# Moving a gain vector's load and transpose, one addition and one norm step in a fused attention and feed-forward kernel

## The chip, the cores and the metric

The kernel runs on one core of a Trainium2 chip. The metric is the device time of one execution in microseconds (us); a change of this kernel's time by less than 0.3% can't be told from none. The core has five instruction streams that run beside each other, each in its own order: the tensor engine (PE, with its weight loads listed apart as PEld), the vector engine (DVE), the scalar engine (ACT), GpSimd (POOL) and the sync engine (SP), which here only issues transfers; SPq is SP's queue of such issues. Semaphores order the streams among each other.

## The reference

Attention with normalised queries and keys is followed by a feed-forward block. Shapes: batch 8, 12 heads, sequence 448, head width 64; 3584 tokens, model width 768, inner width 1024.

```python
q_n, k_n = (rmsnorm(q, g_q), rmsnorm(k, g_k))      # x / sqrt(mean(x*x) + 1e-6) * g
scores = q_n @ k_n.T / sqrt(64)
attn = softmax(scores)
x = (attn @ v)                                     # (B,H,S,D) -> (B*S, H*D)
h = x @ w_in                                       # 768 x 1024
solu = h * softmax(h)
ln = (solu - mean) / sqrt(var + 1e-6) * g_ln
out = ln @ w_out                                   # 1024 x 768
```

The gain `g_ln` is 1024 numbers. The kernel multiplies it into `w_out` when it prepares that matrix, which is long after the attention stage has begun.

## The kernel before, in words

The work has three stages: attention, the product with `w_in` (L982), and the product with `w_out` (L1177). All that the change touches lies in the attention stage and, of that, in its first 75 us.

**Pairs and quads.** Two heads of one batch entry are a pair; there are 48 pairs, numbered from 0, and pairs 2m and 2m+1 (a and b in the code) make quad m. Each pair passes through these steps:

- `load(n)` (L634) fetches the pair's queries and keys by eight transfers on SP's queue; `load_v(m)` (L647, L651) fetches the values of a quad by three. Five buffers hold queries and keys.
- `squares(n)` (L656, ACT), `row_sums(n)` (L664, DVE), `fold_sums(m)` (L674, L675, POOL; for a whole quad) or `fold_one(n)` (L684, L685, DVE; for the early pairs), `rsqrt_seed` (L694, L695, ACT), `rsqrt_step` (L701 to L704, DVE), `normalise(n)` (L713, POOL), `qk_transpose(n)` (L723, DVE) and `gain(n)` (L727, ACT) turn them into the transposed, normalised operand qkT. This row of steps is called the chain of norms below. It goes from engine to engine, and it belongs to the quad after the one that the tensor engine is working on.
- `scores(n, kc)` (L812, PE) makes one block of scores for both heads, and `exponentials` (L802, ACT) takes its exponentials. A quad has seven such units: three of pair a, here called s0, s1 and s2; one for the last 64 keys of both pairs (`scores_last`, L825), here called last; and three of pair b, here called b0, b1 and b2.
- `add(n)` (L839, DVE) adds two of a pair's blocks of exponentials, so that the sums of rows cost fewer matmuls.
- `values_last` and `values` (L854, L865, PE) multiply with the values, `sums(m)` (L884, PE) adds up the exponentials, `inverse(m)` (L895, L896 on DVE, L903 on POOL) takes the reciprocals, and `divide(m)` (L910, L911, DVE) scales the result into `xo`, which `store_x` (L916) sends to memory.

**What sets the order.** The order is written by hand: the code runs under `manual_schedule`, and every engine executes its instructions in the order in which they are recorded. `unit(f)` records f and then whatever `later(...)` has made due. Three banks of the tensor engine's result memory (tag "t") are handed out in turn to the score units, to the sums sm and to the transpose pg below, so each of these must wait until the third one before it has been read.

**The gain vector.** `load_norm_gain()` issues two transfers on SP's queue (L469, 2 KB each) into `grow`. `norm_gain()` transposes `grow` on the tensor engine (L476, one matmul into a bank pg of tag "t") and copies the result to `gcol` on ACT (L477). Before the change the transfers are the last thing that quad 0 records, behind `load(6)`, `load(7)` and two transfers of `w_in` (L510); `norm_gain()` stands in quad 1 behind s1 and ahead of s2.

Of the kernel before, what the change touches and what calls it, by code (L numbers as in the profile page):

```python
# [366 lines left out]
def fast_path(  # L367
# [99 lines left out]
    def load_norm_gain():  # L467
        for i in range(2):
            nc.sync.dma_start(  # L469
                grow[i * HF : (i + 1) * HF].rearrange("c (g j) -> c g j", g=4),  # L470
                moe_g_ln.rearrange("(h g c j) -> h c g j", h=2, g=4, j=32)[i],
            )

    def norm_gain():
        pg = ps_t.tile([P, KF], FP32, tag="t", name="pg")
        nc.tensor.transpose(pg, grow, ident[0:KF, 0:KF])  # L476
        nc.scalar.copy(gcol[:, 0:KF], pg)  # L477
# [149 lines left out]
    def load(n):  # L627
        b, hp = divmod(n, NP)
        h0 = 2 * hp
        d = st[n] = {}  # L630
        d["qk"] = loads.tile([P, 2, NB, 32], FP32, tag="qk", name="qk", bufs=5)
        for s, src in enumerate((q, k)):
            for g in range(4):
                nc.sync.dma_start(  # L634
                    d["qk"][g * 32 : g * 32 + 32, s],
                    src[b, h0 + g // 2].rearrange("(b t) (x d) -> x t b d", t=32, x=2)[g % 2],
                )
# [15 lines left out]
    def squares(n):  # L653
        d = st[n]
        d["sq"] = work.tile([P, 2 * NB, 32], FP32, tag="sq", name="sq", bufs=2)
        nc.scalar.activation(d["sq"], d["qk"].rearrange("p s b d -> p (s b) d"), AF.Square)  # L656
# [3 lines left out]
    def row_sums(n):  # L660
        m, i = divmod(n, 2)
        if i == 0:
            norms[m] = {"part": small.tile([P, 2, 2 * NB], FP32, tag="part", name="part", bufs=2)}
        nc.vector.tensor_reduce(norms[m]["part"][:, i], st[n]["sq"], AX, OP.add)  # L664
# [139 lines left out]
    def scores(n, kc):  # L804
        d = st[n]
        s = ps_t.tile([P, 2, 512], FP32, tag="t", name="s")

        for c in range(0, P, D):
            for h in range(2):
                hh = slice(h * D, (h + 1) * D)  # L810
                keys = slice(NJ * c + kc, NJ * (c + D - 1) + kc + 1, NJ)
                nc.tensor.matmul(  # L812
                    s[c : c + D, h, 0:S], d["qkT"][hh, 1, keys], d["qkT"][hh, 0, :],
                    start=True, stop=True,
                )
        exponentials(d, kc, s)
# [19 lines left out]
    def add(n):  # L836
        d = st[n]
        d["es"] = work.tile([P, 2, S], FP32, tag="es", name="es")
        nc.vector.tensor_tensor(d["es"], d["E", 0], d["E", 1], OP.add)  # L839
# [433 lines left out]
    def unit(f, steps=4):  # L1273
        nonlocal now
        f()
        now += steps
        due = [x for x in todo if x[0] <= now]
        todo[:] = [x for x in todo if x[0] > now]
        for _, g in sorted(due, key=lambda x: x[0]):
            g()  # L1280
# [35 lines left out]
    load(3)  # L1316
    load_v(0)
    load(4)
    load(5)
    with tc.manual_schedule():  # L1320
        warm_up()
# [18 lines left out]
        for m in range(NQ):  # L1340
            a, b = 2 * m, 2 * m + 1

            def outputs():
                values_last(m)
                values(a)


            next1 = m + 1 < NQ
            next2 = m + 2 < NQ
            next3 = m + 3 < NQ  # L1350
            if m == 0:
                unit(lambda: scores(a, 0))
                normalise_rows(1, 0)
                normalise_rows(1, 1)
                unit(lambda: scores(a, 1))
                unit(lambda: scores(a, 2))
                for s in range(2):
                    transpose_rows(1, s)
                    take_rows(1, s)
                squares(2)  # L1360
                row_sums(2)
                fold_one(2)
                unit(lambda: scores_last(m))
                rsqrt_seed(norms["one", 2])
                rsqrt_step(norms["one", 2])
                normalise(2)
                add(a)
                unit(lambda: scores(b, 0))
                unit(lambda: scores(b, 1))
                unit(lambda: scores(b, 2))  # L1370
                squares(3)
                row_sums(3)
                qk_transpose(2)
                fold_one(3)
                gain(2)
                rsqrt_seed(norms["one", 3])
                add(b)
                rsqrt_step(norms["one", 3])
                normalise(3)
                load_v(1)  # L1380
                load(6)
                load(7)
                for _ in range(2):
                    load_next()
                unit(outputs)
                squares(4)
                row_sums(4)
                qk_transpose(3)
                gain(3)
                unit(lambda: values(b))  # L1390
                unit(lambda: sums(m))
                inverse(m)
                load_norm_gain()
                later(1, lambda m=m: divide(m))
                continue
            early = 2 < m and next1
            if early:
                rsqrt_seed(norms[m + 1])
                rsqrt_step(norms[m + 1])
                normalise(a + 2)  # L1400
                normalise(b + 2)
            for x in joins_at.get(m, ()):
                combine_in(x)
            if next1:
                load_v(m + 1)
            unit(lambda: scores(a, 0))
            store_x(m - 1)
            if early:
                qk_transpose(a + 2)
                if next3:  # L1410
                    load(a + 6)
            unit(lambda: scores(a, 1))
            if m == 1:
                squares(5)
                row_sums(5)
                fold_sums(2)
                norm_gain()
            if m == 2:
                rsqrt_seed(norms[m + 1])
                rsqrt_step(norms[m + 1])  # L1420
                normalise(a + 2)
                normalise(b + 2)
            unit(lambda: scores(a, 2))
            unit(lambda: scores_last(m))
            if m < 2:
                add(a)
            unit(lambda: scores(b, 0))
            if m == 1:
                rsqrt_seed(norms[m + 1])
                rsqrt_step(norms[m + 1])  # L1430
                normalise(a + 2)
                normalise(b + 2)
                load(a + 6)
                load(b + 6)
            if m == 2:
                qk_transpose(a + 2)
                load(a + 6)
            unit(lambda: scores(b, 1))
            if early or m == 2:
                qk_transpose(b + 2)  # L1440
                if next3:
                    load(b + 6)
            if m > 1:
                add(a)
            unit(lambda: scores(b, 2))
            if m == 1:
                qk_transpose(a + 2)
            scarce = m < 5
            if next2:
                squares(a + 4)  # L1450
                if not scarce:
                    squares(b + 4)
                row_sums(a + 4)
            if next1:
                gain(a + 2)
            if m == 1:
                add(b)
                qk_transpose(b + 2)
            if next1:
                gain(b + 2)  # L1460
            if scarce:
                squares(b + 4)
                if m > 1:
                    add(b)
            if next2 and m > 1:
                row_sums(b + 4)
                fold_sums(m + 2)
            if not scarce:
                add(b)
            add_more(a)  # L1470
            add_more(b)
            unit(outputs)
            step(m - 2)
            begin(m)
            step(m - 1)
            if m - 1 in sets:
                load_next()
            unit(lambda: values(b))
            if m == NQ - 1:
                block_sums(0, 0)  # L1480
                block_sums(0, 1)
                load_x(1)
            unit(lambda: sums(m))
            inverse(m)
            if m == 1:
                row_sums(b + 4)
                fold_sums(m + 2)
            if next1:
                later(1, lambda m=m: divide(m))
            if m == NQ - 2:  # L1490
                load_x(0)
                sizes(0)
# [191 lines left out]
```

## Time and profile before

| quantity | value |
|---|---|
| median of 3 runs | 831.3 us (830.87 to 833.21) |
| profiled execution, time | 830.15 us |
| profiled execution, span from first to last instruction | 827.9 us |
| mean granted clock of the tensor engine | 0.988 |
| PE busy | 800.3 us (97% of the span) |
| DVE, ACT, POOL busy | 671.0, 460.8, 463.8 us |
| quad 0's scores begin | 10.54 us |
| quads 1, 2, 3, 4: the first score unit begins | 26.18, 53.37, 67.52, 81.32 us |
| quads 1, 2, 3: L865 begins | 46.68, 60.83, 74.63 us |

The span is a little shorter than the profiled execution's own time; the 2.25 us between them lie before the first instruction and after the last. The last two rows of the table are starts of instructions in the timeline. From quad 4 on one quad takes 12.9 us. A timeline's row gives the start and the length in us, the engine, the line and operation, the tile written and read, the number of instructions merged into it, and in brackets how long the engine was idle before it and what ended that.

### The profile page before, as it was taken

What the parts mean: (1) busy time and instruction counts of PE and PEld (TensorE: products, weight loads), DVE (VectorE), ACT (ScalarE), POOL (GpSimd) and SP (SyncE); (2) the same over time, 40 slices, a digit from 0 to 9 for tenths busy, and PEclk for the clock granted to TensorE, in tenths of its full rate; (3) what the DMA queues carried; (4) which work ended last, traced back from release to release, by engine and by line L of the source; (5) the groups of instructions that cost most, each with busy time, mean ns of one, the idle gap of its engine ahead of it and who ended that gap; (6) DMA issues with size and microseconds to landing.
All of it is one profiled execution on the core that took longest, in us unless ns stands there. A gap on an engine that the chain in (4) does not pass through costs nothing.

```text
span 827.9 us, 14945 instructions
## 1 busy us (share of the span) xinstructions
PE 800.3 (97%) x5030; PEld 471.0 (57%) x5030; DVE 671.0 (81%) x1203; ACT 460.8 (56%) x757; POOL 463.8 (56%) x635
## 2 busy tenths in 40 slices
PE   8399999999999999999999999999899999999996
PEld 4133444444444444444444444444589999999996
DVE  5558988888788788579999999998996866966945
ACT  6377877778777786355656534443324464464420
POOL 1243465555555556523254358777477777877761
PEclk9799999999999999999999999999999999999999
DMA  7755878778777762434555444452457466375312
GB/s 136 179 105 117 200 157 193 150 164 182 150 182 157 155 140 84 127 90 127 151 138 169 127 121 115 119 151 74 133 172 239 139 225 222 126 248 192 133 58 82
DMA packets 271938, 122.74 MB, mean 148 GB/s; under 512 B 190444, under 2 KB 257004, under 8 KB 271852
## 3 DMA queue, kind: packets, MB, share of 16 engines
q1 hardware_dynamic: 256668, 111.79, 51.4%
q10 hardware_dynamic: 15184, 9.90, 4.2%
q8 instruction: 42, 0.69, 0.4%
q14 instruction: 44, 0.36, 0.1%
HBM read 84.94 MB, written 36.70 MB: 147 GB/s over the span
## 4 chain that ended last, share of the span: by engine, by line
PE 88%; DVE 4%; SPq 2%; POOL 2%; DMA 2%; issue 1%; ACT 0%; DVEq 0%; POOLq 0%
PE b L982 31%; PE A L1177 14%; PE o L865 12%; PE s L812 12%; PE B L1177 7%; PE sm L884 5%; PE C L1177 3%; PE s L825 2%; PE o L854 2%; SPq L634 2%; DMA grow<-in_moe_g_ln_dram 1%; DVE part L664 0%; POOL sums L1156 0%; DMA x<-in_k_dram 0%; POOL qkn L713 0%
## 5 line engine op out<-in xcount | busy, mean ns | idle before, releaser
L982 PE MATMUL b<-w_in,xg 128*128 128x512 f32 x336 | 151.2, 592 | 0.0
L802 ACT ACTIVATE E<-s 128x896 f32<-128x896 f32 x168 | 139.2, 935 | 17.6 <-PE s L812 16.6
L812 PE MATMUL s<-qkT 64*64 64x448 f32 x1152 | 121.6, 549 | 1.6 <-ACT E L802 0.9
L982 PE MATMUL b<-w_in,xsum 128*128 128x512 f32 x252 | 115.0, 592 | 0.0
L865 PE MATMUL o<-E,v 128*64 128x448 f32 x576 | 113.5, 543 | 0.0
L982 PEld LDWEIGHTS b<-w_in,xg 128*128 128x128 f32 x336 | 63.8, 190 | 80.2 <-issue 76.9
L713 POOL TENSOR_TENSOR qkn<-qk,ny 128x896 f32<-128x896 f32 x46 | 78.0, 1715 | 31.2 <-DVE ny L704 12.0
L674 POOL COPY ss<-part 32x56 f32<-32x56 f32 x88 | 42.6, 484 | 90.6 <-DVE part L664 87.7
L1177 PE MATMUL A<-w_out,sums 128*128 128x192 f32 x392 | 81.1, 330 | 4.0 <-ACT u L1189 2.6
L812 PEld LDWEIGHTS s<-qkT 64*64 64x64 f32 x1152 | 48.5, 163 | 60.1 <-ACT E L802 29.1
L982 PEld LDWEIGHTS b<-w_in,xsum 128*128 128x128 f32 x252 | 47.9, 190 | 60.3 <-issue 57.4
L1060 POOL TENSOR_TENSOR he<-he,mhalf 128x1 f32<-128x1 f32 x28 | 17.1, 610 | 114.5 <-DVE he L1059 112.4
L865 PEld LDWEIGHTS o<-E,v 128*64 128x64 f32 x576 | 39.2, 137 | 72.7 <-issue 67.5
L1177 PE MATMUL B<-w_out,sums 128*128 128x192 f32 x392 | 79.8, 326 | 0.0
L1066 ACT ACTIVATE u<-u,shift,he 128x1024 f32<-128x1024 f32 x28 | 34.7, 1240 | 74.5 <-POOL shift L1062 71.9
L1177 PEld LDWEIGHTS A<-w_out,sums 128*128 128x128 f32 x392 | 67.0, 192 | 5.3 <-issue 2.9
L1177 PEld LDWEIGHTS B<-w_out,sums 128*128 128x128 f32 x392 | 66.1, 190 | 0.2
L839 DVE TENSOR_TENSOR es<-E 128x896 f32<-128x896 f32 x48 | 52.5, 1096 | 0.5 <-ACT E L802 0.5
L723 DVE STREAM_TRANSPOSE qkT<-qkn 128x896 f32<-128x896 f32 x46 | 48.6, 1089 | 5.0 <-POOL qkn L713 5.0
L664 DVE TENSOR_REDUCE part<-sq 128x28 f32<-128x896 f32 x46 | 48.3, 1081 | 4.7 <-ACT sq L656 2.7
L563 POOL TENSOR_TENSOR w_out<-w_out 128x384 f32<-128x384 f32 x44 | 50.7, 1158 | 1.9
L1177 PE MATMUL A<-w_out,s 128*128 128x192 f32 x224 | 46.3, 330 | 0.6 <-ACT u L1189 0.6
(143 smaller groups left out, 1497.4 us busy)
## 6 DMA issues: line engine op xcount, KB each, us to landing
ur<-ud SPq DMA_DIRECT2D x60, 256.0 KB, 4.8
ud<-ub SPq DMA_DIRECT2D x112, 128.0 KB, 2.2
xd<-xo SPq DMA_DIRECT2D x24, 448.0 KB, 4.4
qk<-in_q_dram SPq DMA_DIRECT2D x184, 56.0 KB, 2.3
qk<-in_k_dram SPq DMA_DIRECT2D x184, 56.0 KB, 2.2
v<-in_v_dram SPq DMA_DIRECT2D x24, 384.0 KB, 4.8
out_dram<-P SPq DMA_DIRECT2D x21, 384.0 KB, 3.9
raw<-in_moe_w_in_dram SPq DMA_DIRECT2D x12, 512.0 KB, 4.8
```

The lines of the kernel that those rows point to most:

```text
L563: nc.gpsimd.tensor_tensor(o, p, q, OP.subtract)
L664: nc.vector.tensor_reduce(norms[m]["part"][:, i], st[n]["sq"], AX, OP.add)
L674: e.tensor_copy(ss[g * 32 : g * 32 + 32], part[o * 32 : o * 32 + 32])
L713: e.tensor_tensor(d["qkn"], d["qk"].rearrange("p s b d -> p (s b) d"), y.rearrange("p b -> p b ()").to_broadcast([P, 2 * NB, 32]), OP.mult,)
L723: nc.vector.transpose(d["qkT"].rearrange("p s t -> p (s t)"), d["qkn"].rearrange("p b d -> p (b d)"))
L802: nc.scalar.activation(d["E", kc], s[:, :, 0:S], AF.Exp)
L812: nc.tensor.matmul(s[c : c + D, h, 0:S], d["qkT"][hh, 1, keys], d["qkT"][hh, 0, :], start=True, stop=True,)
L839: nc.vector.tensor_tensor(d["es"], d["E", 0], d["E", 1], OP.add)
L865: nc.tensor.matmul(d["o"][h * D : (h + 1) * D, :], quads[n // 2]["v"][:, n % 2 * 2 + h, kc], d["E", kc][:, h], start=False, stop=(kc == NJ ...
L884: nc.tensor.matmul(sm[g : g + 32, :], ones[:, w], e[:, h, t * S // 2 : (t + 1) * S // 2], start=(x == 0), stop=(x == len(terms) - 1),)
L982: nc.tensor.matmul(o, a[:, c], w_in[i][:, c], start=(c == 0), stop=(c == HD - 1))
L1177: nc.tensor.matmul(k[bank], a[:, c].rearrange("p a i -> p (a i)"), w_out[:, area, i, c], start=begin and c == 0, stop=c == KC - 1, skip_gr ...
```

## The change

It has three parts. First, the two transfers of `g_ln` are issued behind `load(4)` and ahead of `load(5)` (pair 5 is the sixth pair), and `norm_gain()` is recorded behind s2 of quad 1 instead of ahead of it. Second, in quad 0 the addition of the second pair, `add(b)`, is recorded ahead of `row_sums(3)` and no longer between `rsqrt_seed` and `rsqrt_step` of pair 3. Third, in quad 2 the norms of quad 3 (`rsqrt_seed`, `rsqrt_step` and two `normalise`) are recorded behind s2 instead of ahead of it.

```diff
@@ -1316,6 +1316,7 @@
     load(3)
     load_v(0)
     load(4)
+    load_norm_gain()
     load(5)
     with tc.manual_schedule():
         warm_up()
@@ -1369,12 +1370,12 @@
                 unit(lambda: scores(b, 2))
                 squares(3)
+                add(b)
                 row_sums(3)
                 qk_transpose(2)
                 fold_one(3)
                 gain(2)
                 rsqrt_seed(norms["one", 3])
-                add(b)
                 rsqrt_step(norms["one", 3])
                 normalise(3)
@@ -1390,7 +1391,6 @@
                 inverse(m)
-                load_norm_gain()
                 later(1, lambda m=m: divide(m))
                 continue
@@ -1414,13 +1414,14 @@
                 squares(5)
                 row_sums(5)
                 fold_sums(2)
-                norm_gain()
+            unit(lambda: scores(a, 2))
             if m == 2:
                 rsqrt_seed(norms[m + 1])
                 rsqrt_step(norms[m + 1])
                 normalise(a + 2)
                 normalise(b + 2)
-            unit(lambda: scores(a, 2))
+            if m == 1:
+                norm_gain()
             unit(lambda: scores_last(m))
```

No instruction is added or removed: each engine has the same instructions as before, in another order.

## The prediction

> **What bounds the kernel.** The page comes first. PE is busy 97% of the span and holds 88% of the chain of waits; of the 40 slices only the second, 20.7 to 41.4 us, stands at 3 tenths. So PE sets the end, and what the change can bring is PE's idle time in that slice. The waits view gives that hole its cause, and PE's timeline its place:
>
> ```profile
> PE pg L476 <- DMA grow<-in_moe_g_ln_dram: 12.0, 1, 12.0
> ```
>
> ```profile
> 26.18 1.77 PE L812 MATMUL s<-qkT 64*64 64x448 f32 x16
> 39.99 0.24 PE L476 MATMUL pg<-ident,grow 8*128 8x8 f32 x1 [12.05 <-DMA grow<-in_moe_g_ln_dram]
> 40.16 1.77 PE L812 MATMUL s<-qkT 64*64 64x448 f32 x8
> 41.71 1.72 PE L825 MATMUL s<-qkT 64*64 64x448 f32 x8
> ```
>
> PE ends s1 of quad 1 at 27.95 and stands for 12.05 us before a transpose of 0.24 us. The first row has 16 matmuls in the time in which the third has 8: PE comes back at half speed. The chain of waits says why the transfer is late, and the windows view what the clock did:
>
> ```profile
> 34.75 0.36 SPq L510
> ...
> 35.55 4.30 DMA grow<-in_moe_g_ln_dram
> ```
>
> ```profile
> 28.00:32.00 4.00, 0.00 (x0) 0.00 (x0) 2.63 (x5) 2.61 (x4) 0.97 (x5) 0.79 0.69 112
> 36.00:40.00 4.00, 0.01 (x1) 0.04 (x1) 0.19 (x1) 0.00 (x0) 0.82 (x4) 0.50 0.89 304
> 43.00:44.00 1.00, 1.00 (x12) 0.30 (x8) 0.00 (x0) 0.48 (x1) 0.00 (x0) 0.53 0.67 107
> 44.00:46.00 2.00, 2.00 (x28) 0.92 (x24) 0.00 (x0) 1.83 (x5) 0.00 (x0) 1.00 0.54 91
> ```
>
> SP's queue issues without a pause, so the gain's two transfers leave only at 35.17 to 35.84 and land at 39.85. The third number from the end is the granted clock: finer windows put its fall to 0.50 at 30.3 and its return at 43.9.
>
> The hole isn't worth 12 us, though, because the chain of norms for quad 2 runs through it on the other engines:
>
> ```profile
> 34.78 1.82 POOL L674 COPY ss<-part 32x56 f32<-32x56 f32 x4 [3.73 <-DVE part L664]
> 36.68 0.30 POOL L675 TENSOR_TENSOR ss<-ss,part 128x56 f32<-128x56 f32 x1
> ```
>
> ```profile
> 45.39 0.33 ACT L694 ACTIVATE ny<-ss,eps 128x56 f32<-128x56 f32 x1
> 45.75 0.25 ACT L695 ACTIVATE ny<-ny 128x56 f32<-128x56 f32 x1
> ```
>
> The sums ss are there at 36.98, and ACT takes them at 45.39 only because L694 stands behind exponentials whose scores PE hadn't made. With PE early, L694 can move up to ss and no further. That is what is late next.
>
> **Part 2, the addition, and what it starts.** Two rows of DVE:
>
> ```profile
> 21.52 1.09 DVE L664 TENSOR_REDUCE part<-sq 128x28 f32<-128x896 f32 x1 [1.62 <-ACT sq L656]
> ...
> 24.52 1.08 DVE L839 TENSOR_TENSOR es<-E 128x896 f32<-128x896 f32 x1
> ```
>
> The second of three exponentials that begin at 18.14 ends near 19.9, so the addition fits between 19.9 and 21.0 in the idle 1.62 us and delays nothing. Gone from 24.52, it frees two things. The second half of sm waited 0.58 us for it (PE at 25.66), so s0 and s1 run 25.6 to 27.35. And pair 3's L702, held until 25.80, follows L695 (ends 25.22) at 25.25: 0.55 earlier. `normalise(3)` goes from 26.51 to 25.96, `qk_transpose(3)` to 27.69, and L895, which frees sm's bank, ends at 29.10 instead of 29.65. POOL's row names a v transfer as what ended its wait for `normalise(3)`; that transfer is recorded behind it, so L704, ended 0.08 us before, is the releaser. If v were it, this step would come 0.67 later instead of 0.55 earlier.
>
> **Part 1, the transfer and the transpose.** Two issues of 0.67 us together move ahead of 29 others (`load(5)`, v of quad 1, `load(6)`, `load(7)`, two of w_in), which each leave 0.67 later; from v of quad 2 on SP is where it was. Leaving at 18.5 to 19.2, with the 4.30 us of the old landing, `grow` is there at 23.5; it is wanted at 30.4. The delayed loads have room: issued until 24.1, 30.2 and 34.8 and landing some 2.3 us later (page, part 6), they are wanted by `squares` at 31.0, 38.6 and 44.3. Were the room gone, each would cost its 0.67.
>
> Quad 1 then runs like this, with the durations of its own rows. s2 needs sm's bank: 29.15 to 30.1. The exponentials of s0 and s1 follow `gain(3)` on ACT, 0.55 earlier than before, and end at 30.3 and 31.15. pg needs s0's bank, runs at 30.4, and nothing on PE waits for its result. last needs s1's bank: 31.2 to 32.1. ACT does `squares(5)` until 31.95 and s2's exponential until 32.8; so b0 32.8, b1 33.6, b2 34.35. L865 begins at 36.0, against 46.68: **PE is 10.7 us ahead**.
>
> The chain of norms: `divide(0)` and `row_sums(5)` shift with L895 by 0.55 (33.10), the fold with them, ss is there at 36.43, L694 starts at 36.46 against 45.39: **8.9 us ahead**. In front of it ACT idles some 1.8 us; behind it stand the exponentials of b1 and b2 (37.0 to 38.7), which `values(3)` wants from 39 on. `normalise(4)` begins at 37.9 (46.84 before). I keep 1.82 us for the fold's copies, the neighbouring addition on DVE being the same; in quad 2 the same four take 1.03 beside other neighbours, so the other end is 0.8 better.
>
> **How the two shifts meet.** In quad 1 `add(3)` ends at 42.7, sm wants it at 42.3: PE waits 0.45, quad 2's scores begin at 43.15 (10.2 ahead). There ACT still has `gain(5)` and `squares(7)` and begins the exponentials at 45.2 (9.2 ahead). **Part 3** now counts: before, s2's exponential stood behind L694, and b1 waited 0.93 us for it:
>
> ```profile
> 58.33 1.82 PE L812 MATMUL s<-qkT 64*64 64x448 f32 x16 [0.93 <-ACT E L802]
> ```
>
> Now it ends at 47.76, and ss of quad 3 comes at 47.88, so L694 is hardly delayed by standing behind it. b1 starts at 47.8, but the exponential of last stands behind L694 and L695, so b2 starts at 49.4 and L865 at 51.0 (60.83 before: 9.85 ahead). L713 of quad 3's norms starts at 50.0 (58.98: 8.95 ahead). In quad 3 ss is there at 60.0 (69.0), the first exponential ends at 61.45, and last, held for a bank, starts at 61.5 instead of 70.51: 9.0 ahead, PE having waited 1.0 us there instead of 0.47. Now all engines are 9.0 us ahead, and behind quad 3 nothing in the chain of waits differs. Part 3 alone is worth 0.8 us in quad 2, which this meeting eats: I count it 0, between 0 and 0.8.
>
> SP must follow. It issues `load(8)` by about 43 and `load(9)` by 47.5, landing near 50; `squares(8)` and `squares(9)` want them at 51.7 and 55.1. A quad's issues take SP about 10.3 us (16 of 0.51, v 1.7, xd 0.4) against PE's 12.9, so SP, which was the late one, catches up by quad 4.
>
> **The clock, rule against row.** The Trainium skill, "TensorE: Matmul & The Clock Gate", Part 1, has the clock halved after at least one idle window of about 3.4 us and restored after one busy window. By that rule the remaining holes (27.35 to 29.15, then 0.3, 0.6 and 0.7 us around pg, last and b0) are too short, and the clock stays at 1. By the row it fell at 30.3, 2.35 us after the last matmul ended, in a stretch of 3.4 us in which PE still had worked 1.1; the new stretch from 26.9 to 30.3 would have about 1.4. I can't exclude the fall. If it comes and lasts 3.4 us, b2 and L865 are some 0.4 us later; if 6.8 us, about 2 us later. But PE has 1.7 us in hand over the norms, so the sum becomes 9.0 or about 8.7. Rule and row are 0.3 us apart; I take 9.0.
>
> **Sum.** 830.15 - 9.0 = 821.15 us for a profiled execution. The median before is 1.15 above that execution: 831.3 - 9.0 = 822.3.
>
> **Rivals.**
>
> PE's lead is kept. If the fold's copies fall to 1.03 us and DVE makes up the rest in quad 2, all of 10.7 stays: 820.6. For it: quad 2's fold. Against: the addition beside it is the same, and DVE has nearly no idle time in quad 2. Chance 0.13.
>
> The half clock lasts, or a delayed load holds one step up. Half speed until about 41 us costs PE 4 us, of which 1.7 are covered: 6.7 stay, 824.6. For it: the row of the fall. Against: the holes are broken up by work. Chance 0.14.
>
> The wait changes its name: another late thing stands where the gain stood (a load of pair 5, ss), and the gain stays below 2.5 us: about 830. Against it, everything else in the hole had ended by 37. Chance 0.03.
>
> Slower. PE's small stalls keep the clock at half beyond quad 1. At half speed PE loses 0.5 us per us, so the 9.0 are eaten once the half clock lasts 18 us longer than costed, and if it went on through quads 2 and 3 (28 us, 14 lost) the time would be 836. Against: after the old hole it came back within 3.9 us of work. Chance 0.02.
>
> **Numbers.** The forecast has 0.68: its own range, from the clock's 8.7 and the fold's 9.8 and the runs' spread (830.87 to 833.21), is 821.2 to 824. With the next two rivals the range is 820.3 to 824.7. A measurement tells 0.3%, 2.5 us, from no change: faster 0.95, same 0.03, slower 0.02.
>
> **What would show it.** pg no longer waits for a transfer; PE idles about 1.8 us before s2; ACT waits for POOL's ss before L694 in quad 1, which starts near 36.5; L865 of quads 1 and 2 start near 36.0 and 51.0, quad 4's scores near 72.3; the span is near 819. Wrong would be: a DMA named before L656 or L713, L694 far from ss, or a clock of 0.5 beyond 37 us.

## The result, and the profile after

The change makes the kernel faster: 822.85 us (median of 4 executions, 821.82 to 824.16) against 831.09 us for the kernel before on the same chip (830.66 to 833.21). The ratio is 0.9897, with a 95% interval of 0.9874 to 0.9919. The predicted time was 822.3 us, in a range of 820.3 to 824.7. A second set of six executions of the changed kernel, on another chip, has a median of 823.92 us (823.00 to 825.72), 0.9908 of the kernel before there: also within the range, but 1.6 us above the predicted time.

The profiled execution after took 821.82 us, 8.33 less than the one before. Its span is 819.3 us (827.9 before: 8.6 less), and what lies around the span grew by 0.27. Quad 4's scores begin at 72.72 instead of 81.32, which is the same 8.6: all of the gain lies in the first 73 us. From there to the first matmul of L982 both profiles take 256.55 us. One part of the 8.6 is luck of the execution: the first loads landed 0.35 earlier, so quad 0 starts at 10.19 instead of 10.54. Counted from quad 0's start, quad 4 comes 70.78 before and 62.53 after, 8.25 earlier. From here on starts are compared in this way where it says "from quad 0".

The timeline of the kernel after, the rows that answer to the hole in quad 1 and to the chain of norms:

```profile
25.03 1.77 PE L812 MATMUL s<-qkT 64*64 64x448 f32 x16
29.59 1.59 PE L812 MATMUL s<-qkT 64*64 64x448 f32 x8 [2.79 <-DVE r L895]
31.12 0.27 PE L476 MATMUL pg<-ident,grow 8*128 8x8 f32 x1
31.61 1.77 PE L825 MATMUL s<-qkT 64*64 64x448 f32 x8 [0.22 <-ACT E L802]
...
36.45 4.73 PE L865 MATMUL o<-E,v 128*64 128x448 f32 x24
36.57 0.30 POOL L675 TENSOR_TENSOR ss<-ss,part 128x56 f32<-128x56 f32 x1
36.90 0.34 ACT L694 ACTIVATE ny<-ss,eps 128x56 f32<-128x56 f32 x1 [1.65 <-POOL ss L675]
```

The 12.05 us are gone. pg waits for no transfer, L865 of quad 1 starts at 36.45 instead of 46.68, and L694 now waits in ACT for POOL's sums, which end at 36.87, and starts 0.03 behind them: it was at 45.39 and had been held by exponentials. What is left of the hole is 2.79 us ahead of s2, until L895 has read sm's bank.

The windows view of the kernel after; the third number from the end is the granted clock:

```profile
28.00:32.00 4.00, 2.19 (x13) 0.76 (x17) 2.74 (x5) 2.72 (x4) 0.86 (x5) 0.74 0.72 119
32.00:36.00 4.00, 4.00 (x40) 1.31 (x32) 3.53 (x5) 3.04 (x5) 1.25 (x3) 0.84 0.67 108
36.00:40.00 4.00, 4.00 (x28) 1.46 (x22) 0.85 (x4) 3.04 (x5) 2.39 (x4) 1.00 0.85 219
```

The clock fell once more and came back sooner: finer windows have it at 0.50 from 29.9 to 33.3, where it had been at half until 43.9.

### The profile page after: what moved, and what is told of

Read it like the earlier page. It is cut to its first block, busy times and chain, and to the rows that moved or that the text cites. A ratio compares the mean times of both kernels' runs of the same rounds, so it can differ in the third digit from the quotient of the medians.

```text
span 819.3 us, 14945 instructions
## 1 busy us (share of the span) xinstructions
PE 800.6 (98%) x5030; PEld 470.2 (57%) x5030; DVE 672.4 (82%) x1203; ACT 461.0 (56%) x757; POOL 463.6 (57%) x635
## 4 chain that ended last, share of the span: by engine, by line
PE 88%; DVE 3%; SPq 3%; POOL 2%; DMA 2%; issue 1%; ACT 0%; DVEq 0%; POOLq 0%
PE b L982 31%; PE A L1177 14%; PE o L865 12%; PE s L812 12%; PE B L1177 7%; PE sm L884 5%; PE C L1177 3%; SPq L634 3%; PE s L825 2%; PE o L854 2%; DMA v<-in_v_dram 1%; DMA qk<-in_k_dram 0%; POOL sums L1156 0%; POOL qkn L713 0%; POOL sums L1155 0%
## 5 line engine op out<-in xcount | busy, mean ns | idle before, releaser
L982 PE MATMUL b<-w_in,xg 128*128 128x512 f32 x336 | 151.1, 592 | 0.0
L982 PE MATMUL b<-w_in,xsum 128*128 128x512 f32 x252 | 115.0, 592 | 0.0
L865 PE MATMUL o<-E,v 128*64 128x448 f32 x576 | 113.5, 543 | 0.0
L982 PEld LDWEIGHTS b<-w_in,xg 128*128 128x128 f32 x336 | 63.8, 190 | 80.2 <-issue 77.1
L982 PEld LDWEIGHTS b<-w_in,xsum 128*128 128x128 f32 x252 | 47.9, 190 | 60.3 <-issue 57.4
L865 PEld LDWEIGHTS o<-E,v 128*64 128x64 f32 x576 | 39.2, 137 | 72.7 <-issue 65.7
L1066 ACT ACTIVATE u<-u,shift,he 128x1024 f32<-128x1024 f32 x28 | 34.7, 1239 | 74.9 <-POOL shift L1062 72.3
```

The costliest lines, as they stand in the source:

```text
L865: nc.tensor.matmul(d["o"][h * D : (h + 1) * D, :], quads[n // 2]["v"][:, n % 2 * 2 + h, kc], d["E", kc][:, h], start=False, stop=(kc == NJ ...
L982: nc.tensor.matmul(o, a[:, c], w_in[i][:, c], start=(c == 0), stop=(c == HD - 1))
```

## What went wrong inside a right number

Counted from quad 0, L694 of quad 1 moved by 8.14 us (34.85 to 26.71), where 8.93 had been worked out. The 0.79 between them come from one place, the addition of pair 1. The timeline of the kernel after around it:

```profile
18.47 3.59 DVE L839 TENSOR_TENSOR es<-E 128x896 f32<-128x896 f32 x2
18.63 2.48 POOL L713 TENSOR_TENSOR qkn<-qk,ny 128x896 f32<-128x896 f32 x1 [12.00 <-DMA qk<-in_k_dram]
...
21.98 1.07 DVE L664 TENSOR_REDUCE part<-sq 128x28 f32<-128x896 f32 x1
...
26.40 1.70 POOL L713 TENSOR_TENSOR qkn<-qk,ny 128x896 f32<-128x896 f32 x1 [5.29 <-DMA qk<-in_k_dram]
```

The two additions take 1.08 and 2.53 us, not 1.08 each, and the second has filled the gap and more. Beside them POOL multiplies pair 2 (`normalise(2)`), for 2.48 us, where the same multiplication for pair 3 takes 1.70. The trace of before had the sign of it, in two rows that the prediction didn't read together:

```profile
18.81 1.08 DVE L839 TENSOR_TENSOR es<-E 128x896 f32<-128x896 f32 x1
18.98 2.48 POOL L713 TENSOR_TENSOR qkn<-qk,ny 128x896 f32<-128x896 f32 x1 [12.01 <-DMA qk<-in_k_dram]
```

POOL's multiplication begins while DVE's addition has some 0.9 us to go, and takes 0.78 longer than its fellow. In the kernel after the roles are then changed: DVE's second addition is recorded right behind, finds POOL at work, and ends at 22.06, 0.95 after POOL's end at 21.11. These rows fit two instructions that exclude each other, the second standing until the first is through. It did not wait for its operands, for all three exponentials of the pair are done at 20.30:

```profile
17.79 2.51 ACT L802 ACTIVATE E<-s 128x896 f32<-128x896 f32 x3
```

Even behind the last of them an addition of 1.08 us would have ended at 21.38.

## The experiments

All runs are shown in one table. "Quad 4" is the start of its scores from quad 0's start; "to L982" is from there to the first matmul of L982; both come from one profiled execution each. The median of before was 830.95 to 831.48 in the same sets of runs.

| run | median us (executions) | ratio to before, 95% interval | quad 4 | to L982 |
|---|---|---|---|---|
| before, first profile | 831.09 | | 70.78 | 256.55 |
| changed, first profile | 822.85 (4) | 0.9897, 0.9874 to 0.9919 | 62.53 | 256.55 |
| transfers alone | 822.33 (4) | 0.9885, 0.9869 to 0.9902 | 62.28 | 260.0 |
| all but the transfers | 831.53 (10) | 0.9998, 0.9989 to 1.0008 | 71.42 | 256.5 |
| without the addition | 824.04 (4) | 0.9912, 0.9887 to 0.9936 | 62.82 | 256.6 |
| without the third norms | 823.66 (4) | 0.9897, 0.988 to 0.9913 | 62.51 | 260.1 |
| addition behind the row sum | 824.04 (1) | single execution, no interval | 62.75 | 259.0 |
| sums of quad 2 earlier | 823.01 (4) | 0.9894, 0.987 to 0.9918 | 62.66 | 257.7 |
| the same, old addition | 824.43 (4) | 0.9919, 0.9897 to 0.9941 | 62.68 | 256.5 |
| sums and norms earlier | 824.75 (4) | 0.9908, 0.9872 to 0.9945 | 61.55 | 260.0 |
| changed again | 823.92 (6) | 0.9908, 0.989 to 0.9927 | 62.49 | 260.0 |
| w_in and stores on ACT | 837.68 (6) | 1.007, 1.0051 to 1.0089 | 66.85 | 268.6 |
| both of the last kinds | 838.05 (6) | 1.0081, 1.0059 to 1.0103 | 69.56 | 265.2 |
| vl on ACT | 845.14 (5) | 1.0155, 1.0138 to 1.0173 | 62.50 | 280.7 |

**Which part brings the gain.** The first run moves the two transfers of `g_ln` alone, against the kernel before:

```diff
     load(4)
+    load_norm_gain()
     load(5)
...
                 inverse(m)
-                load_norm_gain()
                 later(1, lambda m=m: divide(m))
```

> Only the two transfers of g_ln move; transpose, addition and third quad's norms stay where they were before. Theory (the chain of norms sets what is gained, so the earlier transfer alone brings all of it): pg waits for no transfer, L694 of quad 1 starts near 36.7 us, quad 4's scores begin at 72.3 to 72.9 (72.72 in the changed kernel, 81.32 before), time 822.3 to 823.3. Rival (the transpose must stand behind s2, and the other two parts carry their share): pg ahead of s2 and the old order of the additions cost 1 to 2 us, quad 4's scores at 73.7 or later, time 824 or more.

The median is 822.33 us: the transfers alone bring all of the gain, and the intervals of this run and of the change overlap. In the profile pg stands ahead of s2 as before and waits for sm's bank, not for the transfer. The second run has everything else of the change and the transfers and pg in their old places:

```diff
     load(4)
-    load_norm_gain()
     load(5)
...
                 inverse(m)
+                load_norm_gain()
...
                 fold_sums(2)
+                norm_gain()
             unit(lambda: scores(a, 2))
...
-            if m == 1:
-                norm_gain()
```

> The addition and the third quad's norms move, the transfer and the transpose stay as before. Theory: PE still waits some 12 us for the transfer until about 40 us, and both other parts are hidden behind that wait: quad 4's scores near 81.3, time 830.5 to 831.5, no change. Rival (the early addition or the norms have a worth of their own): 0.5 us or more faster, quad 4's scores at 80.8 or earlier.

```profile
PE pg L476 <- DMA grow<-in_moe_g_ln_dram: 13.9, 1, 13.9
```

This is its waits view (us in total, times, longest). The hole is back, 1.8 us longer than before, because s0 and s1 end 1.1 us earlier and pg comes 0.8 later (40.76); the time is that of before. The other two parts, with the transfer late, are worth nothing.

**The addition.** Two runs move it alone, the rest as changed: back to its old place, and to just behind the row sum.

```diff
-                add(b)
                 row_sums(3)
...
                 rsqrt_seed(norms["one", 3])
+                add(b)
```

> As the changed kernel, but with the addition of pair 1 where it was before. Theory (in its new place the addition stands still until POOL has finished normalise(2), and so holds up the row sum behind it by 0.5 us): the addition lasts 1.08 us instead of 2.53, normalise(3) on POOL begins 0.2 us earlier relative to quad 0 than in the changed kernel, quad 4's scores 0.0 to 0.3 us earlier, time the same within 0.5 us. Rival (as predicted: the addition in its new place is free and brings the norms forward by 0.55): quad 4's scores 0.5 us later than in the changed kernel.

```diff
-                add(b)
                 row_sums(3)
+                add(b)
                 qk_transpose(2)
```

> As the changed kernel, but with pair 1's addition directly behind row_sums(3), when POOL has no work, instead of directly ahead of it, when POOL has normalise(2). Theory (a DVE addition of two tiles and POOL's multiplication stand still for each other): the addition lasts 1.08 us, as everywhere else, and normalise(2) on POOL keeps the 2.48 us that it owes to pair 0's addition. Rival (the addition lasted 2.53 us because its second block of exponentials was late, or because it follows another addition): still well over 1.1 us.

The timeline of the run with the addition behind the row sum:

```profile
18.50 1.08 DVE L839 TENSOR_TENSOR es<-E 128x896 f32<-128x896 f32 x1
18.67 2.48 POOL L713 TENSOR_TENSOR qkn<-qk,ny 128x896 f32<-128x896 f32 x1 [12.00 <-DMA qk<-in_k_dram]
21.22 1.09 DVE L664 TENSOR_REDUCE part<-sq 128x28 f32<-128x896 f32 x1 [1.63 <-ACT sq L656]
22.22 1.08 DVE L839 TENSOR_TENSOR es<-E 128x896 f32<-128x896 f32 x1
```

With POOL through at 21.15 the second addition takes 1.08 us again, and the row sum begins 0.76 earlier than in the changed kernel. In the run with the old place it takes 1.08 too. So the 2.53 us belong to the place beside POOL's multiplication. This run does not separate POOL from the other thing that changed with the place, namely that the addition follows another addition at once; for POOL speaks that its own row is 0.78 us too long in every one of these profiles, in that of before beside a single addition. From quad 0, `normalise(3)` starts at 15.97 in the kernel before, 15.96 with the addition in its old place under the changed rest, 16.21 in the change and 16.43 with the addition behind the row sum. **Moving the addition delays the norms by 0.24 us; the prediction had them 0.55 earlier.** In the run with the old place the clock lay at half for 6.8 us, from 31.3 on, L865 of quad 1 came 28.22 from quad 0 (26.26 after), and quad 4 0.3 later, not earlier, so the expectation failed there. The run of the transfers alone has the addition in its old place too and kept the full clock: in it L694 of quad 1 and quad 4 both come 0.25 earlier than in the change. Why a fall of the clock hides this is worked out below.

**The third part.** The norms of quad 3 go back ahead of s2 in quad 2:

```diff
+            if m == 2:
+                rsqrt_seed(norms[m + 1])
...
             unit(lambda: scores(a, 2))
-            if m == 2:
-                rsqrt_seed(norms[m + 1])
...
```

> As the changed kernel, but with quad 3's norms ahead of s2 in quad 2, as before. Theory: b1 of quad 2 waits about 0.8 us longer, but quad 3's norms, not PE, set the end there, so quad 4's scores stay at 72.6 to 72.9 and the time within 0.3 us of the changed kernel. Rival (the reordering is worth what b1 waited): quad 4's scores 0.8 us later, at 73.5.

The timeline of this run, at b1 of quad 2:

```profile
49.78 1.82 PE L812 MATMUL s<-qkT 64*64 64x448 f32 x16 [1.42 <-ACT E L802]
```

The wait is there, 1.42 us at b1, where the changed kernel has 0.33 ahead of last and 0.61 ahead of b2. And it costs nothing: quad 4 comes at 62.51 from quad 0 against 62.53. What PE loses here it loses in quad 3 otherwise, where last waits 0.36 us in this run and 0.96 in the change.

**Is it the chain of norms?** If L694 of quad 1 sets the gain, then a chain begun earlier must bring more, until PE itself is the bound. One run computes the row sums of pair 5 and the fold of quad 2 before the divisions, with the rest as changed; a second has the old place of the addition besides.

```diff
                 qk_transpose(3)
+                squares(5)
                 gain(3)
...
                 inverse(m)
+                row_sums(5)
+                fold_sums(2)
                 later(1, lambda m=m: divide(m))
...
-            if m == 1:
-                squares(5)
-                row_sums(5)
-                fold_sums(2)
```

> As the changed kernel, but squares(5) is recorded ahead of gain(3), and row_sums(5) and fold_sums(2) directly behind inverse(0), ahead of the division of quad 0; so the sums of quad 2's norms are ready before PE has made the scores that stand in front of L694. Theory (quad 2's norms, not PE, limit what is gained): L694 of quad 1 starts 2 us earlier or more, at some 24.7 us behind the start of quad 0's scores instead of 26.7, quad 4's scores 1.5 to 2.2 us earlier, time 820.5 to 821.5. Rival (PE itself, its banks or its clock, is the bound in quads 1 to 3): L694 moves, quad 4's scores do not by more than 0.5 us.

> As the run with early sums, but with pair 1's addition where it was before the change. Theory: like the run with early sums within 0.3 us, better by up to 0.3 if the clock does as well. Rival (the early addition has a worth once the norms are out of the way): 0.5 us or more slower.

Of the first of the two, the windows and then the timeline:

```profile
32.00:36.00 4.00, 4.00 (x24) 1.30 (x24) 2.81 (x5) 2.40 (x5) 0.48 (x2) 0.50 0.72 110
36.00:40.00 4.00, 4.00 (x30) 1.27 (x24) 1.55 (x4) 3.18 (x6) 2.63 (x2) 0.83 0.89 285
```

```profile
31.16 1.01 POOL L674 COPY ss<-part 32x56 f32<-32x56 f32 x4
...
35.93 0.33 ACT L694 ACTIVATE ny<-ss,eps 128x56 f32<-128x56 f32 x1
...
38.43 4.73 PE L865 MATMUL o<-E,v 128*64 128x448 f32 x24
```

The sums are there at 32.56, and the four copies of the fold take 1.01 us, since no addition of DVE lies beside them (1.82 in the change). L694 comes 1.2 us earlier, no longer held by ss but by the exponentials ahead of it. Nothing is won: the clock lay at half from 30.5 to 37.3, L865 came 1.8 us later from quad 0 than in the change, and PE was the bound. The second run reads the same (L694 25.33, L865 28.07 from quad 0); its median is 1.4 us longer, with intervals that overlap. So both expectations failed, and these two show the other bound, at 62.7.

Put beside each other, the profiles show both bounds (starts from quad 0, in us):

| profile | L694 of quad 1 | L865 of quad 1 | quad 4 | quad 4 behind L694 | quad 4 behind L865 |
|---|---|---|---|---|---|
| transfers alone | 26.46 | 25.40 | 62.28 | **35.82** | 36.88 |
| changed | 26.71 | 26.26 | 62.53 | **35.82** | 36.27 |
| without the third norms | 26.70 | 27.07 | 62.51 | **35.81** | 35.44 |
| changed again | 26.69 | 27.54 | 62.49 | **35.80** | 34.95 |
| sums of quad 2 earlier | 25.55 | 28.05 | 62.66 | 37.11 | **34.61** |
| the same, old addition | 25.33 | 28.07 | 62.68 | 37.35 | **34.61** |
| without the addition | 26.45 | 28.22 | 62.82 | 36.37 | **34.60** |

In the first four PE's path moves by 2.1 us and quad 4 doesn't follow it: it keeps its distance from L694. In the last three it keeps its distance from L865. Quad 4 thus comes at the later of L694 + 35.8 and L865 + 34.6; the kernel before stands 34.64 behind its L865. By this, PE had 1.65 us in hand in the change, where the prediction had 1.7.

The third run moves `rsqrt_seed`, `rsqrt_step` and both `normalise` of quad 2 up too, behind s2 of quad 1, so that L694 follows ss; the addition is in its old place:

```diff
-            if m == 2:
+            if m == 1:
+                norm_gain()
+            if m in (1, 2):
                 rsqrt_seed(norms[m + 1])
...
-                rsqrt_seed(norms[m + 1])
-                rsqrt_step(norms[m + 1])
-                normalise(a + 2)
-                normalise(b + 2)
                 load(a + 6)
```

> As the run with early sums and the old addition, and quad 2's norms (rsqrt_seed, rsqrt_step, two normalise) are recorded behind the transpose pg in quad 1, instead of behind b0. Theory: the norms then lie behind PE's path, so quad 4's scores come another 0 to 1 us earlier than with early sums alone, and what is left is PE's own path: its waits for banks in quad 1. Rival (L694 now stands ahead of the exponentials of last and b0 and holds them up): no earlier, or later.

Here the clock stayed full, and L694 came 4.7 us earlier than in the change, L865 of quad 1 1.1 earlier. Quad 4 is 1.0 earlier, the only run that gets below 62.2, and neither bound holds it (L694 + 35.8 gives 57.8, L865 + 34.6 gives 59.8). It is less than the norms have won, and the timeline says who takes it back in quad 2:

```profile
46.24 0.62 DVE L911 TENSOR_TENSOR xo<-o,r 128x448 f32<-128x448 f32 x1 [1.75 <-DMA xd<-xo]
...
50.45 0.95 ACT L656 ACTIVATE sq<-qk 128x896 f32<-128x896 f32 x1 [1.22 <-DMA qk<-in_k_dram]
```

Now a store that has not left and a load that has not come are the late ones: SP's transfers. The chain of norms sets the gain of the change, as predicted; in this run, 1 us ahead of that, waits for SP's transfers appear.

**What SP does later.** The profile of this run then loses 3.5 us between quad 4 and L982, and so do three others of the table, each with quad 4 within 0.3 us of the change. One of these is the changed kernel itself, run once more:

> The changed kernel itself, for its spread on the same chip. Theory: median 822 to 823.5, single times from 821.5 to 825, the long ones with squares that wait for transfers between 80 and 330 us.

Its waits from 80 to 330 us, then its timeline:

```profile
ACT sq L656 <- DMA qk<-in_k_dram: 6.5, 5, 2.1
```

```profile
199.14 0.95 ACT L656 ACTIVATE sq<-qk 128x896 f32<-128x896 f32 x1 [2.05 <-DMA qk<-in_k_dram]
...
202.26 0.59 PE L884 MATMUL sm<-es,ones 128*32 128x224 f32 x8 [0.27 <-DVE es L839]
205.82 0.98 PE L825 MATMUL s<-qkT 64*64 64x448 f32 x8 [0.52 <-ACT E L802]
...
225.99 0.95 ACT L656 ACTIVATE sq<-qk 128x896 f32<-128x896 f32 x1 [1.68 <-DMA qk<-in_k_dram]
232.66 0.98 PE L825 MATMUL s<-qkT 64*64 64x448 f32 x8 [0.52 <-ACT E L802]
```

The expectation was a median of 822 to 823.5 us and single times up to 825; both are exceeded, and the waits are where it had them. The squares wait for a load, everything behind them on ACT and DVE slides, and the tensor engine gets its sums and exponentials late. By the starts of its L884 four quads take 13.55, 14.32, 13.95 and 13.25 us instead of 12.90, together 3.5 us. The profile of before has no such wait at all, the first profile of the change one of 0.4 us. The same kernel thus gives 821.82 us and 825.72 us, with quad 4 equally early in both. That SP falls behind is seen in the first profile too. From store to store (77.42, 90.68, 103.73, 117.89, 132.80), short waits of its own included, it takes 13.26, 13.05, 14.16 and 14.91 us in quads 4 to 8, against the tensor engine's 12.9. In the profile of before the same four are 12.90, 12.89, 13.16 and 12.80 (from 85.96), with at most 1.0 us of a quad spent waiting for `xo`. So SP kept step before and had little to spare; in the change the eight issues behind a store take 5.96, 5.78 and 5.90 us in quads 4 to 6, where they took 5.58, 5.29 and 5.44. Why they take longer the runs don't settle.

Three runs tried to take work from SP. The first puts the transfers of `w_in` and the stores on ACT's queue, the second has the early sums and norms besides, and the third moves only the two small transfers of `vl`, from quad 4 on:

```diff
-            nc.sync.dma_start(to, w[c * P : (c + 1) * P])
+            nc.scalar.dma_start(to, w[c * P : (c + 1) * P])
...
-        nc.sync.dma_start(
+        (nc.sync if m == NQ - 1 else nc.scalar).dma_start(
...
-            store_x(m - 1)
...
+            store_x(m - 1)
```

> As the changed kernel, but the w_in transfers (L510) are issued on ACT instead of SP, and so is store_x of all quads but the last, recorded behind b2 instead of behind s0. Theory (since PE is 8 us earlier, SP's queue runs without a pause and some executions lose 1 to 4 us in quads 5 to 20 to loads that come just too late): between 80 and 330 us no square waits for a transfer, from quad 4's scores to the first matmul of L982 it takes 256.5 us as in the undisturbed executions, and the times lie closer together, 821.5 to 823. Rival (the spread comes from somewhere else, or what is bound are the DMA engines and not the queue's order): squares wait as before, the spread stays 2 us or more, or the two issues per quad cost ACT what they save.

> As the run with early sums and norms, with the same two transfers moved to ACT. Theory: division 1 no longer waits for store 0, squares(8) not for load(8), so what the early norms gain in quads 1 and 2 lasts: quad 4's scores at 60 to 61 us behind the start of quad 0's (62.5 in the changed kernel), 256.5 us from there to L982, time 819.5 to 821. Rival: as before, a later wait takes it back, time 822.5 or more.

```diff
-        for i in range(2):
-            nc.sync.dma_start(d["vl"][i * D : (i + 1) * D], src[2 * i : 2 * i + 2, NJ * P : S].rearrange("h p d -> p h d"))
+        if m < 4:
+            load_vl(m, nc.sync)
...
+            unit(lambda: scores(a, 1))
+            if early:
+                load_vl(m + 1, nc.scalar)
                 if next3:
                     load(a + 6)
-            unit(lambda: scores(a, 1))
```

> The changed kernel; from quad 4 on the two small transfers of vl (L651 in the changed kernel) are issued by ACT behind s1 of the quad before, and no longer by SP. Theory (SP's issuing, some 13 us a quad against the tensor engine's 12.9, decides whether the squares find their loads): SP is relieved of 1.3 us a quad, in the profile the squares (ACT, square of q and k) wait for loads under 1 us in all between 80 and 330 us, the time from quad 4's scores to the first product with w_in is 256.5 us (260.0 in two profiles of late loads), the median is near 822 and no execution lies above 823.5. Rival (the transfers themselves are late, whoever issues, since their engines are 75% busy): nothing changes, profile and single times spread as before over 821.8 to 825.7 with a median of 823 to 824. Second rival, as with the transfers of w_in and xo on ACT: [...]PE loses 0.5 us or more a quad, 20 quads, 833 us or more.

All three are slower than before, and the expectation of the theory failed in each; the last fits the time of its second rival, 833 us or more. The waits of SP's queue, first with `w_in` and the stores on ACT (14 to 110 us), then with `vl` on ACT (80 to 345 us):

```profile
SPq L469 <- DMA raw<-in_moe_w_in_dram: 9.9, 1, 9.9
SPq L651 <- DMA xd<-xo: 4.3, 1, 4.3
```

```profile
SPq L634 <- DMA vl<-in_v_dram: 26.2, 20, 3.9
```

SP has fewer issues and more waits: it stands until transfers of ACT's queue have landed, 20 times for `vl` alone. ACT issues at its own place in its stream: `vl` of one quad 8.9 us behind its v (162.79 and 153.91), where SP had issued it 0.43 behind. In the first of the three SP stands 9.9 us in the middle of the two gain transfers, `load(5)` is issued from 30.39 (20.73 in the change), and the squares of pair 5 wait 4.08 us for it. In the run with `vl` the squares wait 24.7 us in all between 80 and 345, and PE loses 24.1 us between quad 4 and L982. That the late loads come from SP's late issues fits these profiles; that less work for SP would cure them is not shown, since no run gave SP less time to spend.

## The prediction, step by step

**Right.** PE's hole sets the bound, its 12 us aren't the gain, and the chain of norms is what is late next: L694 starts 0.03 behind ss, as worked out. L865 of quad 1 was put at 36.0 and came at 36.45, L694 at 36.46 and 36.90, add(3)'s wait at 0.45 and 0.39, last in quad 3 at 61.5 and 61.91 with a wait of 1.0 and 0.96, quad 4 at 72.3 and 72.72, the span at 819 and 819.3. The transfers and the delayed loads landed in time. Part 3 counted for 0 and is worth 0.

**Wrong: "the addition fits between 19.9 and 21.0 in the idle 1.62 us and delays nothing".** It took 2.53 us there. The step asked only whether DVE was idle; POOL's multiplication, whose own row read 2.48 us where its neighbour's read 1.70, was not looked at. The 0.55 us that the step puts on `normalise(3)`, and so on L694, are a loss of 0.24. These 0.79 us are as much as the whole difference at L694 (8.93 to 8.14), and they cover that at quad 4, 9.0 predicted and 8.25 measured from quad 0. That the total hides it is luck, for the execution after had its first loads 0.35 earlier: 8.33 in all, and the predicted 822.3 lies 0.55 below the median. The Trainium skill has the rule that was missed, in "SBUF — State Buffer", "Who interferes with whom": a VectorE instruction with two inputs in SBUF and a GpSimd instruction that reads SBUF share one read interface, and whichever has it locks the other out. The rows agree: 2.53 us for 1.08, and 2.48 for 1.70. By this rule the addition, ready behind POOL's start, ends 1.08 us behind POOL's end, at 22.19, and measured is 22.06.

**Wrong: "a quad's issues take SP about 10.3 us ..., so SP, which was the late one, catches up by quad 4".** It takes 13.05 to 14.91 us there, and took 12.8 to 13.2 before. The sum had each of the 16 issues at 0.51 us, and left out the weight transfer's 0.48: the first four behind v's and the store's take 3.3 to 3.9 us together, the second four 2.1 to 2.7 and only the later fours 2.0 to 2.4. In quads 2 and 3 it didn't matter; later it costs up to 3.5 us in some executions. The gain that is left is inside the range.

**The clock.** Row and rule were weighed, and the rule was taken: clock at 1. The row was right. It fell in the change at 29.9, at the end of 2.8 us without a matmul. It cost nothing: from s2 to L865 of quad 1 the change takes 6.86 us, and 6.85 had been worked out with the full clock. In three other profiles (addition in its old place, and both with early sums) the half clock lasted 6.8 us, L865 came 1.8 to 2.0 us later than in the change, as had been put on a fall of that length, and PE was the bound, as the rival of the lasting half clock had it, though only by 0.1 to 0.3 us of quad 4. In the second profile of the changed kernel it lasted 6.8 us too, from 29.1; L865 came 1.3 us later, and quad 4 no later: this PE had in hand.

The rivals "PE's lead is kept" and "the wait changes its name" fell with the rows above: PE waits in quads 2 and 3 (0.33, 0.61, 0.96 us), and nothing took the place of the transfer. The slower case didn't come.

## What to carry to other kernels

An idle gap on one engine is not yet room: look at what the other engine that reads the same memory does in that gap, and read a row that is longer than its fellows of the same shape (2.48 against 1.70) as a sign of it before placing anything there. A hole of 12 us is worth what the next late chain leaves of it, and that can be worked out from the trace to within a few tenths by asking for every wait who ends next. When the whole moves forward by 8 us, read each queue's time from one iteration to the next, not from a sum of its issues: one that keeps step with 12.9 us, with 0 to 1 us of waiting in it, has little to give when its transfers take longer.

## What was not expected of the hardware

- DVE's addition of two operands and POOL's multiplication take turns, to within 0.15 us of their full lengths: 1.08 us becomes 2.53, 1.70 becomes 2.48, and the fold's four copies on POOL 1.01 become 1.82 beside an addition.
- The clock fell at the end of 2.8 us without a matmul, and after 2.35 in the profile of before, each time less than the idle window of about 3.4 us that the Trainium skill gives in "TensorE: Matmul & The Clock Gate", Part 1. In the changed kernel the half clock lasted 3.4 us in one profile and 6.8 in the other. After holes of 1.76 us it stayed at 1 in two profiles (transfers alone; sums and norms earlier) and fell in two others (addition in its old place; the same with early sums). The order of the tensor engine's work doesn't decide it alone; what does is open.
- The transfers that were moved to ACT's queue didn't become independent of SP's: SP's issues waited 26.2 us for transfers of ACT's queue. How the two are tied isn't shown by the traces.
- One kernel has executions that differ by 3.9 us (821.82 and 825.72) with the same start of quad 4: whether the loads of later quads come 1 to 2 us late makes the difference from there to L982 (256.55 and 260.0). What tips it is open.
